# Shift columns by a selection matmul, v's shift rows behind the query stage, and the text modulated on its way out of PSUM

## The chip, the core and the metric

The kernel runs on one core of a Trainium2 chip. A core has five engines that work side by side and wait for one another through semaphores: TensorE multiplies matrices (PE in the profile; its loads of the stationary operand are PEld), VectorE (DVE) and ScalarE (ACT) work elementwise, GpSimd (POOL) does elementwise work more slowly and issues DMAs, and SyncE (SP) here issues most DMAs. Operands lie in SBUF, 128 partitions wide; TensorE writes its sums to PSUM, in banks of 512 fp32 values per partition. The metric is the device time of one execution in microseconds (us).

## What is computed

One attention block of a diffusion transformer with two streams, image and text. There are B = 2 batches, Ni = 256 image tokens and Nt = 32 text tokens in each, and D = 1152; all is bfloat16.

```python
mod_i = (_silu(c) @ wmod_img).reshape(B, 6, 1, D)      # only 0, 1, 2 are used
mod_t = (_silu(c) @ wmod_txt).reshape(B, 6, 1, D)
shi, sci, gai = mod_i[:, 0], mod_i[:, 1], mod_i[:, 2]  # shift, scale, gate; text likewise
hi = _layernorm(x_img, axis=-1) * (1 + sci) + shi
ht = _layernorm(x_txt, axis=-1) * (1 + sct) + sht
qkvi = hi @ wqkv_img
qkvt = ht @ wqkv_txt
# q, k, v: text tokens first, then image tokens
scores = jnp.einsum('bqd,bkd->bqk', q, k) * D ** (-0.5)
p = _softmax(scores, axis=-1)
a = jnp.einsum('bqk,bkd->bqd', p, v)
out_i = x_img + gai * (ai @ wo_img)
out_t = x_txt + gat * (at @ wo_txt)
```

## The kernel before, in words

**Tiling.** D is cut into KT = 9 blocks of 128; the 512 image tokens are NIT = 4 row blocks of 128, TPB = 2 for each batch. `hT_i` holds the modulated image tokens transposed (partitions: a block of D; columns: tokens). The text's 64 tokens are one tile, `xn_t`, and `hT_t` transposed.

**Weights.** Twelve blocks of 1152 x 1152 (2592 KB each) are used. They come on SP's queue in the order in which they stand in the code: `w_sc_i` and `w_v_i` in pieces between the rows of x, then `w_sh_i`, `w_q_i` (in thirds along D, `K3`), `w_sh_t`, `w_sc_t`, `w_k_i` (thirds), `x_t`, `w_q_t`, `w_k_t`, `w_ga_i`, `w_v_t`, `w_o_i`, `w_ga_t`, `w_o_t`. Their pool has six buffers that go round: `w_k_i` takes the place of `w_sc_i`, `w_q_t` that of `w_v_i`, `w_k_t` that of `w_sh_i`, `w_ga_i` that of `w_q_i`, and so on. A load is issued when the last reader of the tile that was there is done. SP works its queue in order.

**Stages.** The order of the instructions on each engine is the order of the code.
1. Layer norm of the image rows, transposes, scale. `mod_cols` (L188) makes modulation columns: for each block j of D, nine matmuls with a 128x128 block of weights as the stationary operand and the two columns of silu(c) moving, so 81 matmuls of two columns for all of D.
2. v of the image from hidden states that are scaled but not yet shifted (`v_block`, `v_rest`): v = (scaled x) @ w_v, with the shift's part, shift @ w_v, added to it later (`v_shift`, L393).
3. The shift's columns: `mod_cols(w_sh_i, ...)`, L347, copied to `mod_i` (L348) and, as bfloat16, to `shT32` (L349). `apply_mod` (L203) adds them to `hT_i`, nine slices for each batch, dealt over DVE, ACT and POOL.
4. `mod_rows` (L370) makes rows: the stationary operand is 32 columns wide, `sT32` or `shT32`, so four groups of matmuls share the array side by side (`tile_position`), each with 288 columns of the weights; the result has a row per group and batch, at partitions 32 g + b. The rows are written to DRAM by POOL (L385) and read back broadcast over partitions. For v's shift, `mod_rows(w_v_i, 4, lhs=shT32)` runs ahead of the query projection; the rows come back in `bvb` (L391).
5. `qk_img` (L410) for q and then k of the image: output blocks of 128 in groups, the first three together and then one by one; hooks put other work between groups. `v_shift` stands at block 5 of q. Behind q come the text's shift and scale rows (two `mod_rows`), which POOL reads back broadcast into `mb_t` (L433). In k's stage stand `txt_norm` (block 0), `txt_modulate` (block 5, L449 and L450 with `mb_t`) and `txt_transposes` (block 8; ACT copies the result to `hT_t`, L456).
6. Text q and k (L467), scores, softmax, the image's gate rows, text v, attention (`aps`), and the output projection: `out_chunk` (L643) for four row blocks, and between blocks 2 and 3 the text's gate and output. The output tile `o` has two buffers, and a stored block must land before its buffer is written again.

`evac` (L138) copies PSUM to SBUF in turn by DVE and ACT. Tiles of PSUM are seven buffers of `ps_mm` and one of `ps_sm`.

Of the kernel before, what the change touches and what calls it, by code (L numbers as in the profile page):

```python
# [14 lines left out]
def kernel(  # L15
# [14 lines left out]
    nc = tc.nc  # L30
    bf = mybir.dt.bfloat16
    f32 = mybir.dt.float32
    PSUM = bass.MemoryType.PSUM

    B, NI, D = x_img.shape
    NT = x_txt.shape[1]
    P = 128
    KT = D // P
    NTOK = NI + NT
    NIT = (B * NI) // P  # L40
    TPB = NI // P
    NTT = B * NT
# [8 lines left out]
    NM = 1024  # L51

    const = ctx.enter_context(tc.tile_pool(name="const", bufs=1))
    wpool = ctx.enter_context(tc.tile_pool(name="w", bufs=6))
    act = ctx.enter_context(tc.tile_pool(name="act", bufs=1))
    work = ctx.enter_context(tc.tile_pool(name="work", bufs=2))
    small = ctx.enter_context(tc.tile_pool(name="small", bufs=4))
    ps_mm = ctx.enter_context(tc.tile_pool(name="ps_mm", bufs=7, space=PSUM))
    ps_sm = ctx.enter_context(tc.tile_pool(name="ps_sm", bufs=1, space=PSUM))
# [13 lines left out]
    def load_w(src, c0, ksplits=((0, KT),)):  # L73
        t = wpool.tile([P, KT, D], bf, tag="w")
        for (k0, k1) in ksplits:
            nc.sync.dma_start(t[:, k0:k1, :], w_view(src)[:, k0:k1, c0:c0 + D])
        return t
# [6 lines left out]
    w_v_i = wpool.tile([P, KT, D], bf, tag="w", name="w_v_i")  # L84
# [22 lines left out]
    w_sh_i = load_w(wmod_img, 0)  # L107
    w_q_i = load_w(wqkv_img, 0, K3)


    ident = const.tile([P, P], bf)
# [5 lines left out]
    sT32 = const.tile([P, KT, 32], bf)  # L117
    nc.gpsimd.memset(sT32[:], 0.0)
    shT32 = const.tile([P, KT, 32], bf)
# [8 lines left out]
    sT = const.tile([P, KT, B], bf)  # L128
# [9 lines left out]
    def evac(out_ap, in_ap):  # L138
        if evac_idx[0] % 2 == 0:
            nc.vector.tensor_copy(out_ap, in_ap)  # L140
        else:
            nc.scalar.copy(out_ap, in_ap)
        evac_idx[0] += 1
# [20 lines left out]
    hT_i = act.tile([P, KT, B * NI], bf, tag="Bt")  # L164

    mod_i = const.tile([P, 2 * KT, B], f32, name="mod_img")
# [21 lines left out]
    def mod_cols(wt, out_ps, j0, j1):  # L188
        for j in range(j0, j1):
            for kt in range(KT):  # L190
                nc.tensor.matmul(out_ps[:, j - j0, :], lhsT=wt[:, kt, j * P:(j + 1) * P], rhs=sT[:, kt, :],  # L191
                                 start=(kt == 0), stop=(kt == KT - 1))
# [10 lines left out]
    def apply_mod(kt, t0, t1, shift, eng):  # L203
        b = t0 // TPB
        sl = hT_i[:, kt, t0 * P:t1 * P]
        ap = mod_i[:, kt, b:b + 1] if shift else mod_i[:, KT + kt, b:b + 1]
        op = ALU.add if shift else ALU.mult
        if eng == 0:
            nc.vector.tensor_scalar(sl, sl, ap, None, op0=op)
        elif eng == 1:  # L210
            if shift:
                nc.gpsimd.tensor_scalar(sl, sl, 1.0, ap, op0=ALU.mult, op1=ALU.add)
            else:
                nc.gpsimd.tensor_scalar(sl, sl, ap, 0.0, op0=ALU.mult, op1=ALU.add)  # L214
        elif shift:
            nc.scalar.activation(sl, sl, ACT.Identity, bias=ap, scale=1.0)
        else:
            nc.scalar.activation(sl, sl, ACT.Identity, scale=ap)
# [83 lines left out]
    v_i = act.tile([P, NIT, D], bf, tag="A")  # L302
# [26 lines left out]
    bvb = act.tile([P, B, D], bf)  # L329

    def v_rest(i0, i1):
        ps = ps_mm.tile([P, NIT, P], f32, tag="mm")
        for i in range(i0, i1):
            for kt in range(KT):
                nc.tensor.matmul(ps[:, i - i0, :], lhsT=hT_i[:, kt, i * P:(i + 1) * P], rhs=w_v_i[:, kt, NM:D],  # L335
                                 start=(kt == 0), stop=(kt == KT - 1))
        evac(v_i[:, i0:i1, NM:D], ps[:, 0:i1 - i0, :])

    v_rest(0, TPB)
    ps = ps_mm.tile([P, VW], f32, tag="mm")  # L340
    for kt in range(KT):
        nc.tensor.matmul(ps[:], lhsT=hT_i[:, kt, 3 * P:4 * P], rhs=w_v_i[:, kt, VW:NM], start=(kt == 0), stop=(kt == KT - 1))  # L342
    evac(v_i[:, 3, VW:NM], ps[:])


    mps = ps_sm.tile([P, KT, B], f32, tag="sm")
    mod_cols(w_sh_i, mps, 0, KT)  # L347
    nc.vector.tensor_copy(mod_i[:, 0:KT, :], mps[:])  # L348
    nc.scalar.copy(shT32[:, :, 0:B], mps[:])  # L349
    for kt in range(KT):  # L350
        apply_mod(kt, 0, TPB, True, (0, 1, 2, 0, 2, 1, 0, 0, 2)[kt])
    v_rest(TPB, NIT)

    w_sh_t = load_w(wmod_txt, 0)
    w_sc_t = load_w(wmod_txt, D)
    w_k_i = load_w(wqkv_img, D, K3)
# [7 lines left out]
    w_ga_t = load_w(wmod_txt, 2 * D)  # L364
    w_o_t = load_w(wo_txt, 0, K3)

    NGG = 4
    gsc = tc.dram_tile([5, B, D], bf, name="mod_scratch")

    def mod_rows(w_blk, si, add_one=False, lhs=None):  # L370
        lhs = sT32 if lhs is None else lhs
        gps = ps_mm.tile([P, VC], f32, tag="mm")
        for kt in range(KT):
            for g in range(NGG):
                nc.tensor.matmul(gps[32 * g:32 * g + 32, :], lhsT=lhs[:, kt, :], rhs=w_blk[:, kt, g * VC:(g + 1) * VC],  # L375
                                 start=(kt == 0), stop=(kt == KT - 1), tile_position=(0, 32 * g))
        g_sb = work.tile([P, VC], bf, tag="garow")
        if add_one:
            nc.vector.tensor_scalar_add(g_sb[:], gps[:], 1.0)
        else:  # L380
            evac(g_sb[:], gps[:])
        if si is None:
            return g_sb
        for b in range(B):
            nc.gpsimd.dma_start(gsc[si, b, :].rearrange("(g j) -> g j", g=NGG), g_sb[b:P:32, :])  # L385

    for kt in range(KT):
        apply_mod(kt, TPB, NIT, True, (0, 1, 2, 0, 2, 1, 0, 0, 2)[kt])
    mod_rows(w_v_i, 4, lhs=shT32)
    for b in range(B):  # L390
        nc.gpsimd.dma_start(bvb[:, b, :], gsc[4, b, :].partition_broadcast(P))  # L391

    def v_shift():  # L393
        for i in range(NIT):
            nc.vector.tensor_add(v_i[:, i, :], v_i[:, i, :], bvb[:, i // TPB, :])


    qkT = act.tile([P, 2 * KT, B, NTOK], bf, tag="Q")

# [10 lines left out]
    def qk_img(wq, blk, hooks):  # L410

        groups = [(0, 3)] + [(j, j + 1) for j in range(3, KT)]
        for (j0, j1) in groups:
            if j0 in hooks:
                hooks[j0]()
            pss = [ps_mm.tile([P, B * NI], f32, tag="mm", name="qkps") for _ in range(j0, j1)]
            for kt in range(KT):
                for j in range(j0, j1):
                    nc.tensor.matmul(pss[j - j0][:], lhsT=wq[:, kt, j * P:(j + 1) * P], rhs=hT_i[:, kt, :],  # L419
                                     start=(kt == 0), stop=(kt == KT - 1))  # L420
            for j in range(j0, j1):
                qk_evac(qkT[:, blk * KT + j, :, 0:NI], pss[j - j0][:].rearrange("p (b n) -> p b n", b=B), blk)

    mb_t = act.tile([NTT, 2, D], bf)

    def txt_rows_shift():
        mod_rows(w_sh_t, 0)

    def txt_rows_scale():
        mod_rows(w_sc_t, 1, add_one=True)  # L430
        for k in range(2):
            for b in range(B):
                nc.gpsimd.dma_start(mb_t[b * NT:(b + 1) * NT, k, :], gsc[k, b, :].partition_broadcast(NT))  # L433

    qk_img(w_q_i, 0, hooks={5: v_shift})
    txt_rows_shift()
    txt_rows_scale()

    hT_t = act.tile([P, KT, NTT], bf)

    xn_t = act.tile([NTT, D], bf)

    def txt_norm():
# [1 line left out]
        junk = small.tile([P, 1], f32, bufs=1)  # L445
        nc.scalar.activation(junk[:], eps_t[:], ACT.Exp)

    def txt_modulate():
        nc.vector.tensor_mul(xn_t[:], xn_t[:], mb_t[:, 1, :])  # L449
        nc.vector.tensor_add(xn_t[:], xn_t[:], mb_t[:, 0, :])  # L450

    def txt_transposes():
        tpt = ps_mm.tile([P, KT, NTT], bf, tag="mm")
        for kt in range(KT):
            nc.tensor.transpose(tpt[:, kt, :], xn_t[:, kt * P:(kt + 1) * P], ident[0:NTT, 0:NTT])
        nc.scalar.copy(hT_t[:], tpt[:])  # L456

    qk_img(w_k_i, 1, hooks={0: txt_norm, 5: txt_modulate, 8: txt_transposes})

    FG = 6  # L460
    for blk, wq in enumerate([w_q_t, w_k_t]):
        for j0 in range(0, KT, FG):
            jn = min(FG, KT - j0)
            ps = ps_mm.tile([P, FG, NTT], f32, tag="mm")
            for j in range(j0, j0 + jn):
                for kt in range(KT):
                    nc.tensor.matmul(ps[:, j - j0, :], lhsT=wq[:, kt, j * P:(j + 1) * P], rhs=hT_t[:, kt, :],  # L467
                                     start=(kt == 0), stop=(kt == KT - 1))
            qk_evac(qkT[:, blk * KT + j0:blk * KT + j0 + jn, :, NI:NTOK],
                    ps[:, 0:jn, :].rearrange("p j (b n) -> p j b n", b=B), blk)  # L470


    qpos = [[0, P, 2 * P], [NT, NT + P, 0]]
    rsum = {}
# [18 lines left out]
    def scores_txt_and_gate():  # L493
# [10 lines left out]
        for kt in range(KT):  # L504
            for g in range(NGG):
                c0 = 2 * VC + g * HC
# [6 lines left out]
        for b in range(B):  # L513
            nc.gpsimd.dma_start(gsc[3, b, 0:2 * VC].rearrange("(g j) -> g j", g=2), g_sb[64 + b:P:32, 0:VC])  # L514
            nc.scalar.dma_start(gsc[3, b, 2 * VC:D].rearrange("(g j) -> g j", g=NGG), g_sb[b:P:32, VC:VC + HC])
        return st
# [51 lines left out]
    def attn_out():  # L568
        for dts, own in (((0, 4, 1), 0), ((2, 5, 3), 1), ((6, 8, 7), 1)):
# [6 lines left out]
            for (dt, b, aps) in accs:  # L576
                g, blk = divmod(dt, NGG)
                r = 32 * (2 * (g % 2) + b)
# [43 lines left out]
    def txt_gate():  # L622
        g_sb = mod_rows(w_ga_t, None)
        return g_sb
# [72 lines left out]
    g_sb = txt_gate()  # L697
    pss = out_txt_mm()
# [37 lines left out]
```

## Time and profile before

| | us |
|---|---|
| median of 3 runs | 119.61 (119.52 to 120.07) |
| the profiled execution | 119.72 |
| its span, first to last instruction | 117.9 |
| busy in it: TensorE | 110.8 |
| busy: VectorE, ScalarE, GpSimd | 55.7, 33.0, 26.4 |
| moved by DMA | 41.63 MB, mean 353 GB/s |
| granted clock of TensorE | 1.00 |

The profile is of one execution. Its lines by engine give the busy time; the rows of slices cut the span in 40 equal parts of 2.95 us, with a digit for the busy tenths of each (9 is 90% or more) and, for DMA, the rate. The chain of waits is followed back from the last instruction: each piece has its start, its length and its name (engine, what it writes, line), with xN where N pieces were merged. In the timeline a row has the start, the length, the engine (a q behind it: the engine's instruction queue), the line and the operation, out<-in.

### The profile page before, as it was taken

The page shows a single profiled execution, that of the slowest core. Times are in us where ns is not written, and L with a number is a line of the kernel's source. Part 1 is how long each engine was busy: PE and PEld are TensorE (multiplying, and loading weights), DVE is VectorE, ACT ScalarE, POOL GpSimd, SP SyncE. Part 2 cuts the span into 40 slices and gives each one's busy share as a digit, 9 for nine tenths or more (in the row PEclk, how much of TensorE's full clock was granted, in tenths as well). Part 3 has the DMA queues.
Part 4 walks back from the last instruction along what each step waited for, and adds up shares of the span by engine and source line. Part 5 has one row for each costly group of instructions (what it writes and reads, how often), then busy time and mean ns, then how long its engine had stood idle before and what let it go on. Part 6 is the DMA issues. An engine that isn't in the chain of part 4 may idle for free.

```text
span 117.9 us, 2733 instructions
## 1 busy us (share of the span) xinstructions
PE 110.8 (94%) x1158; PEld 65.1 (55%) x1166; DVE 55.7 (47%) x131; ACT 33.0 (28%) x80; POOL 26.4 (22%) x53
## 2 busy tenths in 40 slices
PE   5858899999999999999999999999999999999990
PEld 1234564546964444455444447978665666667670
DVE  1789910452380221923362270336444778835781
ACT  4538660342090301220073032134533600000200
POOL 4000103700074020007070000002116089900000
DMA  3999999999999999999999999999999999991062
GB/s 77 347 392 349 366 323 382 413 411 412 405 412 407 407 411 413 411 408 334 356 408 402 331 411 413 403 416 399 414 401 411 417 381 399 410 370 49 0 183 67
DMA packets 22807, 41.63 MB, mean 353 GB/s; under 512 B 1231, under 2 KB 6507, under 8 KB 22795
## 3 DMA queue, kind: packets, MB, share of 16 engines
q1 hardware_dynamic: 21696, 39.68, 89.6%
q0 software_dynamic: 768, 1.64, 3.7%
q10 hardware_dynamic: 331, 0.15, 0.5%
q8 instruction: 9, 0.15, 0.5%
q14 instruction: 3, 0.02, 0.1%
HBM read 40.11 MB, written 1.35 MB: 352 GB/s over the span
## 4 chain that ended last, share of the span: by engine, by line
PE 75%; DVE 11%; DMA 9%; issue 1%; ACT 1%; DVEq 0%
PE qkps L419 30%; PE va L230 10%; PE ps L655 8%; DMA out_dram<-o 7%; DVE stats L149 5%; PE aps L573 4%; PE ps L467 4%; PE sps L487 4%; PE gps L375 3%; PE mps L191 3%; DMA x_i<-in_x_img_dram 3%; PE ps L588 2%; PE ps L335 2%; PE ps L342 2%; DVE tmp L662 2%; DVE xn_i L161 1%
## 5 line engine op out<-in xcount | busy, mean ns | idle before, releaser
L419 PE MATMUL qkps<-hT_i,t 128*128 128x512 bf16 x158 | 35.3, 379 | 0.2
L419 PEld LDWEIGHTS <-t 128*128 128x128 bf16 x162 | 15.6, 98 | 19.0 <-issue 0.5
L655 PE MATMUL ps<-t,aT 128*128 128x384 bf16 x99 | 16.4, 326 | 0.0
L230 PE MATMUL va<-w_v_i,hT_i 128*128 128x512 bf16 x60 | 14.1, 379 | 0.8 <-ACT hT_i L179 0.3
L655 PEld LDWEIGHTS <-aT 128*128 128x128 bf16 x117 | 11.1, 98 | 6.7 <-issue 0.2
L230 PEld LDWEIGHTS <-hT_i 128*128 128x128 bf16 x63 | 5.8, 97 | 7.2 <-issue 0.6
L639 POOL TENSOR_TENSOR w_og<-t,gb 128x384 bf16<-128x384 bf16 x9 | 8.7, 997 | 4.4 <-DMA gb<-mod_scratch 4.4
L662 DVE SCALAR_TENSOR_TENSOR tmp<-ps,rs,gb 128x384 bf16<-128x384 f32 x11 | 6.8, 617 | 2.4 <-PE ps L655 2.3
L149 DVE BATCH_NORM_STATS2 stats<-x_i 128x6 f32<-128x384 bf16 x12 | 6.0, 545 | 2.6 <-DMA x_i<-in_x_img_dram 2.6
L405 ACT ACTIVATE qkT<-qkps 128x512 bf16<-128x512 f32 x5 | 2.9, 596 | 14.4 <-PE qkps L419 14.4
L664 DVE TENSOR_TENSOR o<-tmp,x_i 128x384 bf16<-128x384 bf16 x11 | 5.1, 465 | 3.1 <-DMA out_dram<-o 2.7
L385 POOL DMA_DIRECT2D mod_scratch<-g_sb x6 | 3.6, 608 | 12.5 <-DVE g_sb L140 12.5
L214 POOL TENSOR_SCALAR hT_i<-hT_i,mod_img 128x256 bf16<-128x256 bf16 x5 | 2.5, 515 | 16.2 <-ACT rstd L156 9.6
L126 PE MATMUL wps<-wz 128*128 128x512 bf16 x14 | 4.9, 494 | 1.2 <-DVE wz L116 1.2
L403 DVE TENSOR_SCALAR qkT<-qkps 128x512 bf16<-128x512 f32 x4 | 2.7, 686 | 6.5 <-PE qkps L419 6.5
L514 POOL DMA_DIRECT2D mod_scratch<-g_sb x2 | 1.2, 582 | 19.9 <-DVE g_sb L511 19.9
L140 DVE CAST aT<-aps 128x288 bf16<-128x288 f32 x9 | 3.6, 451 | 3.3 <-PE aps L580 3.3
L467 PEld LDWEIGHTS <-t 128*128 128x128 bf16 x162 | 4.9, 98 | 0.2
L573 PE MATMUL aps<-pT,v_i 128*128 128x288 bf16 x36 | 4.9, 287 | 0.0
L467 PE MATMUL ps<-hT_t,t 128*128 128x64 bf16 x162 | 4.9, 193 | 0.0
L631 ACT CAST gbf<-bps 128x288 bf16<-128x288 f32 x2 | 0.7, 402 | 14.8 <-PE bps L629 14.8
L487 PE MATMUL sps<-qkT 128*128 128x288 bf16 x36 | 4.7, 286 | 0.0
(119 smaller groups left out, 135.6 us busy)
## 6 DMA issues: line engine op xcount, KB each, us to landing
t<-in_wmod_txt_dram SPq DMA_DIRECT2D x3, 2592.0 KB, 22.0
t<-in_wmod_img_dram SPq DMA_DIRECT2D x2, 2592.0 KB, 24.3
t<-in_wqkv_img_dram SPq DMA_DIRECT2D x6, 864.0 KB, 15.3
t<-in_wqkv_txt_dram SPq DMA_DIRECT2D x2, 2592.0 KB, 17.5
t<-in_wqkv_txt_dram SPq DMA_DIRECT2D x3, 864.0 KB, 13.5
t<-in_wo_img_dram SPq DMA_DIRECT2D x1, 2592.0 KB, 17.8
t<-in_wo_txt_dram SPq DMA_DIRECT2D x3, 864.0 KB, 15.2
w_sc_i<-in_wmod_img_dram SPq DMA_DIRECT2D x3, 576.0 KB, 7.6
```

What stands on the lines that cost most here:

```text
L126: nc.tensor.matmul(ps[:], lhsT=wz[:, 0:P], rhs=wz[:], start=True, stop=True)
L140: nc.vector.tensor_copy(out_ap, in_ap)
L149: nc.vector.bn_stats(stats[0:np_, k, :], x_ap[:, k * CH:(k + 1) * CH])
L230: nc.tensor.matmul(ps[:], lhsT=hT_i[:, kt, i * P:(i + 1) * P], rhs=w_v_i[:, kt, half * VW:(half + 1) * VW], start=(kt == 0), stop=(kt == K ...
L419: nc.tensor.matmul(pss[j - j0][:], lhsT=wq[:, kt, j * P:(j + 1) * P], rhs=hT_i[:, kt, :], start=(kt == 0), stop=(kt == KT - 1))
L467: nc.tensor.matmul(ps[:, j - j0, :], lhsT=wq[:, kt, j * P:(j + 1) * P], rhs=hT_t[:, kt, :], start=(kt == 0), stop=(kt == KT - 1))
L487: nc.tensor.matmul(sps[:], lhsT=qkT[:, ft, b, q0:q0 + P], rhs=qkT[:, KT + ft, b, :], start=(ft == 0), stop=(ft == KT - 1))
L573: nc.tensor.matmul(aps[:], lhsT=v_i[:, b * TPB + kj, dt * P:(dt + 1) * P], rhs=pTs[b][:, kj, :], start=(kj == 0), stop=False)
L639: nc.gpsimd.tensor_mul(w_og[:, dt, 0:CH], w_o_i[:, dt, NG0:D], gb[:, B - 1, NG0:D])
L655: nc.tensor.matmul(ps[:, 0:cw], lhsT=aT[:, dt, t0:t0 + P], rhs=rhs, start=(dt == DTS[0]), stop=(dt == DTS[-1]))
L662: nc.vector.scalar_tensor_tensor(tmp[:, 0:cw], ps[:, 0:cw], rsum[(b, qi)][:], gb[:, b, cs], op0=ALU.mult, op1=ALU.mult)
L664: nc.vector.tensor_add(o[:, cs], tmp[:, 0:cw], x_i[:, i, cs])
```

## The change

- Shift columns: `rows_for_cols` makes the shift as rows, four groups side by side with 256 columns each, for the first eight blocks of D. An evacuation puts the rows in SBUF (`shr`). `select_cols` then turns rows into columns: the stationary operand is a 128x128 block of `shr`, the moving one is `sel8`, which holds the eight columns of the identity that belong to the rows in use; two matmuls of eight columns. The ninth block's column comes from nine matmuls as before (`last_col`). `cols_out` writes the columns to `mod_i` by two DVE operations.
- Order in front: v's last columns of the second batch come first; those of the first batch stand around the selection, one row block before it and one behind. `apply_mod` takes batch 1 first, then batch 0; q's first group of three blocks goes over the tokens in two cuts, batch 1 and then batch 0. `shT32` is copied by POOL.
- v's shift rows, with their DMAs, come behind the query stage and the text's rows. `v_shift` is done for row blocks 0 and 1 on POOL, placed at block 8 of k, and for 2 and 3 on DVE, behind the text's q and k.
- Text: shift and scale are made as rows and turned into columns too (`txt_cols`, at block 3 of k); the way over DRAM and `mb_t` is gone. The transposes of the normalized text stand at block 5, and DVE multiplies and adds as it moves the result from PSUM to `hT_t`.

The diff, cut:

```diff
-    v_rest(0, TPB)
+    sel8 = const.tile([P, NGG, B], bf)
+    nc.gpsimd.tensor_copy(sel8[:], ident[:].rearrange("p (g r) -> p g r", g=NGG)[:, :, 0:B])
+    def rows_for_cols(wt, nm):
+        gps = ps_mm.tile([P, RC], f32, tag="mm")
+        for kt in range(KT):
+            for g in range(NGG):
+                nc.tensor.matmul(gps[32 * g:32 * g + 32, :], lhsT=sT32[:, kt, :], rhs=wt[:, kt, g * RC:(g + 1) * RC],
+                                 start=(kt == 0), stop=(kt == KT - 1), tile_position=(0, 32 * g))
+        g_sb = work.tile([P, RC], bf, tag=nm, bufs=1, name=nm)
+        evac(g_sb[:], gps[:])
+        return g_sb
+    def last_col(wt, cps):
+        for kt in range(KT):
+            nc.tensor.matmul(cps[:, NCOL:NCOL + B], lhsT=wt[:, kt, (KT - 1) * P:D], rhs=sT[:, kt, :],
+                             start=(kt == 0), stop=(kt == KT - 1))
+    def select_cols(g_sb, cps):
+        for c in range(2):
+            nc.tensor.matmul(cps[:, c * NGG * B:(c + 1) * NGG * B], lhsT=g_sb[:, c * P:(c + 1) * P],
+                             rhs=sel8[:].rearrange("p g b -> p (g b)"), start=True, stop=True)
+    def cols_out(dst, cps, add):
+        nc.vector.tensor_scalar_add(dst[:, 0:KT - 1, :].rearrange("p (g c) b -> p c g b", c=2),
+                                    cps[:, 0:NCOL].rearrange("p (c g b) -> p c g b", c=2, b=B), add)
+        nc.vector.tensor_scalar_add(dst[:, KT - 1, :], cps[:, NCOL:NCOL + B], add)
+    v_rest(TPB, NIT)
...
-    mod_cols(w_sh_i, mps, 0, KT)
-    nc.vector.tensor_copy(mod_i[:, 0:KT, :], mps[:])
-    nc.scalar.copy(shT32[:, :, 0:B], mps[:])
+    shr = rows_for_cols(w_sh_i, "shr")
+    cps = ps_sm.tile([P, NCOL + B], f32, tag="sm")
+    last_col(w_sh_i, cps)
+    psr = ps_mm.tile([P, TPB, P], f32, tag="mm")
+    for i in range(TPB):
+        for kt in range(KT):
+            nc.tensor.matmul(psr[:, i, :], lhsT=hT_i[:, kt, i * P:(i + 1) * P], rhs=w_v_i[:, kt, NM:D],
+                             start=(kt == 0), stop=(kt == KT - 1))
+        if i == 0:
+            select_cols(shr, cps)
+            cols_out(mod_i[:, 0:KT, :], cps, 0.0)
     for kt in range(KT):
-        apply_mod(kt, 0, TPB, True, (0, 1, 2, 0, 2, 1, 0, 0, 2)[kt])
-    v_rest(TPB, NIT)
+        apply_mod(kt, TPB, NIT, True, SHE[kt])
+    evac(v_i[:, 0:TPB, NM:D], psr[:])
+    nc.gpsimd.tensor_copy(shT32[:, :, 0:B], mod_i[:, 0:KT, :])
+    for kt in range(KT):
+        apply_mod(kt, 0, TPB, True, SHE[kt])
...
-    mod_rows(w_v_i, 4, lhs=shT32)
-    for b in range(B):
-        nc.gpsimd.dma_start(bvb[:, b, :], gsc[4, b, :].partition_broadcast(P))
...
+            cuts = [(NI, B * NI), (0, NI)] if blk == 0 and j0 == 0 else [(0, B * NI)]
...
-    qk_img(w_q_i, 0, hooks={5: v_shift})
-    txt_rows_shift()
-    txt_rows_scale()
+    qk_img(w_q_i, 0, hooks={})
+    tsh = rows_for_cols(w_sh_t, "tsh")
+    tsc = rows_for_cols(w_sc_t, "tsc")
+    mod_rows(w_v_i, 4, lhs=shT32)
+    for b in range(B):
+        nc.gpsimd.dma_start(bvb[:, b, :], gsc[4, b, :].partition_broadcast(P))
+    ctp = ps_sm.tile([P, 2, NCOL + B], f32, tag="sm")
+    last_col(w_sh_t, ctp[:, 0, :])
+    last_col(w_sc_t, ctp[:, 1, :])
...
-        nc.vector.tensor_mul(xn_t[:], xn_t[:], mb_t[:, 1, :])
-        nc.vector.tensor_add(xn_t[:], xn_t[:], mb_t[:, 0, :])
...
-        nc.scalar.copy(hT_t[:], tpt[:])
+        nc.vector.tensor_mul(hv, tpt[:].rearrange("p k (b t) -> p k b t", b=B),
+                             mod_t[:, 1, :, :].unsqueeze(3).to_broadcast([P, KT, B, NT]))
+        nc.vector.tensor_add(hv, hv, mod_t[:, 0, :, :].unsqueeze(3).to_broadcast([P, KT, B, NT]))
...
-    qk_img(w_k_i, 1, hooks={0: txt_norm, 5: txt_modulate, 8: txt_transposes})
+    qk_img(w_k_i, 1, hooks={0: txt_norm, 3: txt_cols, 5: txt_transposes, 8: shift_two})
...
+    for i in range(2, NIT):
+        v_shift(i, nc.vector)
```

More of the change, by code (lines that the diff above doesn't have):

```diff
@@ L337, in v_rest @@
         evac(v_i[:, i0:i1, NM:D], ps[:, 0:i1 - i0, :])
-    v_rest(0, TPB)
+    NGG = 4
+    RC = 2 * P
+    sel8 = const.tile([P, NGG, B], bf)
+    nc.gpsimd.tensor_copy(sel8[:], ident[:].rearrange("p (g r) -> p g r", g=NGG)[:, :, 0:B])
+    NCOL = 2 * NGG * B
+    def rows_for_cols(wt, nm):
[20 more added lines that the diff above has]
+    v_rest(TPB, NIT)
     ps = ps_mm.tile([P, VW], f32, tag="mm")
@@ L343 @@
     evac(v_i[:, 3, VW:NM], ps[:])
-    mps = ps_sm.tile([P, KT, B], f32, tag="sm")
-    mod_cols(w_sh_i, mps, 0, KT)
-    nc.vector.tensor_copy(mod_i[:, 0:KT, :], mps[:])
-    nc.scalar.copy(shT32[:, :, 0:B], mps[:])
-    for kt in range(KT):
-        apply_mod(kt, 0, TPB, True, (0, 1, 2, 0, 2, 1, 0, 0, 2)[kt])
-    v_rest(TPB, NIT)
+    shr = rows_for_cols(w_sh_i, "shr")
[9 more added lines that the diff above has]
+            cols_out(mod_i[:, 0:KT, :], cps, 0.0)
+    SHE = (0, 1, 2, 0, 2, 1, 0, 0, 2)
+    for kt in range(KT):
+        apply_mod(kt, TPB, NIT, True, SHE[kt])
[3 more added lines that the diff above has]
+        apply_mod(kt, 0, TPB, True, SHE[kt])
     w_sh_t = load_w(wmod_txt, 0)
@@ L365 @@
     w_o_t = load_w(wo_txt, 0, K3)
-    NGG = 4
     gsc = tc.dram_tile([5, B, D], bf, name="mod_scratch")
@@ L385, in mod_rows, with v_shift @@
             nc.gpsimd.dma_start(gsc[si, b, :].rearrange("(g j) -> g j", g=NGG), g_sb[b:P:32, :])
-    for kt in range(KT):
-        apply_mod(kt, TPB, NIT, True, (0, 1, 2, 0, 2, 1, 0, 0, 2)[kt])
-    mod_rows(w_v_i, 4, lhs=shT32)
-    for b in range(B):
-        nc.gpsimd.dma_start(bvb[:, b, :], gsc[4, b, :].partition_broadcast(P))
-    def v_shift():
-        for i in range(NIT):
-            nc.vector.tensor_add(v_i[:, i, :], v_i[:, i, :], bvb[:, i // TPB, :])
+    def v_shift(i, eng):
+        eng.tensor_add(v_i[:, i, :], v_i[:, i, :], bvb[:, i // TPB, :])
     qkT = act.tile([P, 2 * KT, B, NTOK], bf, tag="Q")
@@ L416, in qk_img @@
             pss = [ps_mm.tile([P, B * NI], f32, tag="mm", name="qkps") for _ in range(j0, j1)]
[L417 to L420, printed above, removed]
+            cuts = [(NI, B * NI), (0, NI)] if blk == 0 and j0 == 0 else [(0, B * NI)]
+            for (t0, t1) in cuts:
+                for kt in range(KT):
+                    for j in range(j0, j1):
+                        nc.tensor.matmul(pss[j - j0][:, t0:t1], lhsT=wq[:, kt, j * P:(j + 1) * P],
+                                         rhs=hT_i[:, kt, t0:t1], start=(kt == 0), stop=(kt == KT - 1))
             for j in range(j0, j1):
                 qk_evac(qkT[:, blk * KT + j, :, 0:NI], pss[j - j0][:].rearrange("p (b n) -> p b n", b=B), blk)
[L424 to L433, printed above, removed]
-    qk_img(w_q_i, 0, hooks={5: v_shift})
-    txt_rows_shift()
-    txt_rows_scale()
+    qk_img(w_q_i, 0, hooks={})
[7 more added lines that the diff above has]
+    last_col(w_sc_t, ctp[:, 1, :])
+    mod_t = const.tile([P, 2, KT, B], f32, name="mod_txt")
     hT_t = act.tile([P, KT, NTT], bf)
@@ L446, in txt_norm, with txt_cols @@
         nc.scalar.activation(junk[:], eps_t[:], ACT.Exp)
-    def txt_modulate():
-        nc.vector.tensor_mul(xn_t[:], xn_t[:], mb_t[:, 1, :])
-        nc.vector.tensor_add(xn_t[:], xn_t[:], mb_t[:, 0, :])
+    def txt_cols():
+        select_cols(tsh, ctp[:, 0, :])
+        select_cols(tsc, ctp[:, 1, :])
+        for k in range(2):
+            cols_out(mod_t[:, k, :, :], ctp[:, k, :], float(k))
     def txt_transposes():
@@ L455, in txt_transposes, with shift_two @@
             nc.tensor.transpose(tpt[:, kt, :], xn_t[:, kt * P:(kt + 1) * P], ident[0:NTT, 0:NTT])
-        nc.scalar.copy(hT_t[:], tpt[:])
-    qk_img(w_k_i, 1, hooks={0: txt_norm, 5: txt_modulate, 8: txt_transposes})
+        hv = hT_t[:].rearrange("p k (b t) -> p k b t", b=B)
+        nc.vector.tensor_mul(hv, tpt[:].rearrange("p k (b t) -> p k b t", b=B),
+                             mod_t[:, 1, :, :].unsqueeze(3).to_broadcast([P, KT, B, NT]))
+        nc.vector.tensor_add(hv, hv, mod_t[:, 0, :, :].unsqueeze(3).to_broadcast([P, KT, B, NT]))
+    def shift_two():
+        for i in range(2):
+            v_shift(i, nc.gpsimd)
+    qk_img(w_k_i, 1, hooks={0: txt_norm, 3: txt_cols, 5: txt_transposes, 8: shift_two})
     FG = 6
```

## The prediction

> **What bounds the kernel now.** First the page: how busy is TensorE, and how busy are the DMA engines, slice by slice?
>
> ```profile
> PE 110.8 (94%) x1158; PEld 65.1 (55%) x1166; DVE 55.7 (47%) x131; ACT 33.0 (28%) x80; POOL 26.4 (22%) x53
> PE   5858899999999999999999999999999999999990
> DMA  3999999999999999999999999999999999991062
> GB/s 77 347 392 349 366 323 382 413 411 412 405 412 407 407 411 413 411 408 334 356 408 402 331 411 413 403 416 399 414 401 411 417 381 399 410 370 49 0 183 67
> ```
>
> Both are full, from about 10 to 106 us. So there are two clocks: the matmuls, and the weights on SP's queue. Which decides is read where the stream ends, in the chain from 93 us on.
>
> ```profile
> 98.84 8.05 DMA out_dram<-o
> 106.99 0.36 DVE o L664
> 108.18 0.47 DVE g_sb L140
> 108.69 0.40 PE bps L629 x2
> ```
>
> The first image row block's store lies behind the last weights and lands at 106.9; DVE needs its buffer, and the gate rows' evacuation stands behind that. But the text matmuls before L629 (36 in 2.25 from 106.22) would have let TensorE go on at about 108.55. So the transfers lead by 0.14 us: a later stream moves the end fully, a later TensorE all but 0.14, and speeding up one of them alone wins at most that.
>
> Next, the chain from 28 to 55 us, where the change works.
>
> ```profile
> 30.02 2.02 PE mps L191 x81
> 32.03 1.03 PE ps L335 x18
> 33.06 1.22 PE gps L375 x36
> 34.28 0.32 PE qkps L419
> ...
> 51.87 2.32 PE gps L375 x72
> ```
>
> No wait appears: the 81 small matmuls for the shift's columns, 18 for v's last columns, 36 for v's shift rows, the query projection, and the text's two sets of rows.
>
> Last, SP's part of the timeline.
>
> ```profile
> 44.97 2.00 SPq L358 DMA_DIRECT2D x_t<-in_x_txt_dram  x1
> 47.07 6.85 SPq L76 DMA_DIRECT2D t<-in_wqkv_txt_dram  x2
> 54.02 7.70 SPq L76 DMA_DIRECT2D t<-in_wmod_img_dram  x1
> ```
>
> SP runs from one issue to the next; it is held by a full queue, not by buffers. w_q_t, issued at 47.07, lands at 64.58.
>
> **TensorE, step by step** (times of this profiled execution: 119.72 us, span 117.9 with 1.8 around it; the median of the runs is 119.61, so the change found is added to that).
>
> Front, from 30.02. Out: 2.02 + 1.03 + 1.22 = 4.27. In:
> - shift rows, 36 matmuls of 256 columns: 1.22 x 256/288 = 1.08.
> - last block's column, 9 x 2.02/81 = 0.22; v's last columns of the first row block, 1.03/2 = 0.5. Together they hide ACT's evacuation (an L142 of 128x256 took 0.36).
> - two selections: nothing like them is in the trace; from 0.05 (two of L191's) to 0.2 (two of the spread, L629, 0.40 for 2 x 288 columns, are dearer). I take 0.1, as they have 8 columns. TensorE is at 31.9.
> - then DVE: two column operations (L348: 0.18) and a shift of 128x256 (L209: 0.29), with three handovers of 0.05: first shifted slice at about 32.75. The second half of v's columns covers 0.5 of it; 0.4 is open. DVE's queue holds nothing else then; POOL (0.55 a slice) and ACT (0.50) keep ahead of the 3 x 0.109 that TensorE needs for a slice.
>
> So the query projection starts at 32.8, not 34.28. Its first three blocks come in two cuts of 27 matmuls of 256 columns (54 x 0.109 against 27 x 0.217: nothing). But it now meets its weights. The second third of w_q_i lands at 33.07; the last one, 885 KB at the 410 GB/s of the page, is due 2.16 later, at 35.2. TensorE asks for it after 18 matmuls, at 34.76: a wait of 0.45, which also swallows whatever is won ahead of it. Then 36 x 0.109 and 54 x 0.217: the query stage ends at 50.9 instead of 51.87, 1.0 early.
>
> Then text shift and scale rows, 2 x 1.03, v's shift rows 1.16, two last columns 18 x 0.025 = 0.46, entry and exit of the column tiling 0.1: 3.8 in place of 2.32. The key projection starts 0.5 later than before. Four selections in it: 0.1. Text transposes stay 0.36, and move three blocks ahead. In all +0.6 (from -0.25, the bare count of matmuls with every wait hidden, to +1.0, with both waits whole and dearer selections); at the end 0.14 less: +0.45.
>
> Edits at no price, with their cover: DVE's multiply and add of the text as it leaves PSUM replace two of 0.75 and ACT's copy of 0.64; three key blocks (6 us) cover them, and without that cover up to 1.5 would show. v's shifts 2 and 3 (L395, 0.75 each) stand on DVE between the last text evacuation (76.8) and the first row maximum (78.1): the maximum is some 0.2 late, but the transposes that follow wait for it only at 83. On POOL, shifts 0 and 1 are priced by L639 (997 ns for 384 columns): 3 us each, after the broadcast rows land near 66, done by 73; POOL's next duty, the gate rows' DMAs, comes at 81.8. The four column operations of the text (0.18 each) take DVE 0.7 near 60, while TensorE has four more PSUM buffers to fill. v's shift rows take their DMAs along: two small writes and two broadcasts of 288 KB, 0.6 each to issue on POOL (L385, L391), which idles there, and whose eight text issues go. shT32's copy moves to POOL, where nothing follows but batch 0's slices, due 3 us later.
>
> POOL's long additions can hold up DVE: L664 takes 357 ns at the least and 750 at the most, beside L639, so 0.4 more against a POOL addition of 1.0. By that row a text add beside a POOL shift costs at most 1.2 more, within the 6 us of cover. A rule speaks against this part: the Trainium skill, "SBUF — State Buffer", section "Who interferes with whom", says that VectorE and GpSimd take a shared port by an exclusive lock and that a tensor_tensor with two SBUF inputs contends; by it the text add could be shut out for a whole shift, which would leave the sum as it is only because of the same cover.
>
> **The transfers.** Out: four loads of text modulation (4 x 72 KB, 0.295 MB at 410 GB/s: 0.7 us). The four small writes ahead of them are nothing. bvb's 0.59 MB (1.4 us) moves from 44-47 to after 60.
>
> The cost is in a buffer. The pool holds six weight tiles, so w_q_t takes w_v_i's place, and w_v_i is read last by v's shift rows: before at 34, now behind the query stage and the text rows, 50.9 + 0.1 + 2.06 + 1.16 = 54.2. SP, whose issue stood at 47.07, waits seven us, and every later weight load is queued behind it. What covers it is the backlog. Summing the bytes of SP's queue in the order of issue, what precedes w_q_t is through at 55.2 now, and at 53.8 with bvb gone from before it. The first packet follows an issue by 0.3 (the store at 111.90: bytes by 112.4) to 1.0 (the first load at 0.74: nothing by 1.70). So the stream restarts at 54.7 to 55.4, dry for 0.9 to 1.6. Less the 0.7 saved: +0.2 to +0.9 at the end; I take +0.5, a little below the middle, since the queue is warm. If engines that lag (landings come 1.3 to 2.3 after the sum of bytes) use the pause to catch up, it is less, down to -0.7 at best.
>
> The Trainium skill, "DMA: Bandwidth & Descriptors", section "Anatomy of one DMA", puts a fixed 2.0 us on a DMA, mostly completion. Here a 32 KB store takes 1.5 from issue to landing, and its first bytes come early, as the page says. Had all 2.0 stood ahead of the bytes, the stream would be 1.7 later.
>
> Both clocks thus lose about half a us; the later one decides, and small waits where they cross (w_ga_i lands at 78.31 for 79.12; w_v_t's last third at 84.76 for 85.35) can add a little: **+0.65, 120.3 us**, from +0.3 to +1.3.
>
> **Rivals.**
> - *The stream falls far behind*: SP released later, or a slow restart; dry for 2.4 rather than 1.3, so +1.7, and TensorE then waits for w_ga_i. 121.3 us, up to 121.6. For it: the margin is thin and every load is behind it. Against: packets of the warm queue came within 0.5 us.
> - *It ends even*: the ring's lag is caught up in the pause, and w_q_i's third lands by 34.8. TensorE then starts the key stage +0.1 to +0.2; +0.2 in all: 119.8. For it: landings vary by 1 us against the bytes.
> - *Not slower but faster*: 70 matmuls fewer in the front and fewer bytes count whole. The place is the handover after the selection: if it hides (the first shifted slice by 32.4 and the weights by 34.3) TensorE gains its bare 0.25, the transfers give 0.7, and the end is 0.14 + 0.25 = 0.4 early: 119.2. Only with the key stage starting before 54.0 does it decide. The landing of w_q_i's third speaks against it; to pass 119.0 more would have to go.
>
> **How the numbers follow.** Forecast 0.50, far behind 0.17, even 0.22, faster 0.11. About 0.5% (0.6 us: below 119.0, above 120.2) is what a measurement can tell. Slower: 0.38 of the forecast's 0.50, whose middle lies just beyond the limit, and all of 0.17: 0.55. Faster: half of the last rival and a little for what I overlooked, 0.07. The rest, 0.38, is the same. The range 119.4 to 121.4 leaves out a tenth on each side.
>
> **What would show it.** Right: SP's w_q_t issue at about 54 with a buffer wait; a slice of GB/s near 54 to 56 below 300; a TensorE wait near 35 for w_q_i; query stage ending near 50.9, key stage starting near 54.7; the first store landing after 107. Wrong: w_q_t issued near 47; a key stage that starts before 54.1; text operations or the late shifts on the chain; an end above 121.4 or below 119.4.

## The result, and the profile after

The changed kernel takes 124.03 us (median of 4 runs, 122.86 to 124.75) against 119.65: 3.1% slower, ratio 1.0312 with a 95% interval of 1.0266 to 1.0357. One of its four runs (124.75) counts as slow, and the ratio leaves it out. 120.3 was forecast, in a range of 119.4 to 121.4. The profiled execution took 122.86, its span is 121.1.

From the page of the kernel after, the rows for busy TensorE, the DMA engines and their rate in 40 slices:

```profile
PE 111.3 (92%) x1173; PEld 67.4 (56%) x1181; DVE 54.9 (45%) x134; ACT 32.8 (27%) x79; POOL 26.9 (22%) x49
PE   5768999999969999999999999999999999997980
DMA  3999999999999999999999999999999999991052
GB/s 88 346 377 337 322 347 380 394 390 390 391 394 385 395 388 389 391 393 292 368 391 397 405 387 394 394 388 390 393 390 390 391 340 392 391 362 60 2 177 68
```

The DMA engines are as busy as before, but a busy slice moves 390 GB/s, where it moved 411. That begins in the eighth slice, near 21 us, where the code of both kernels is still the same: everything up to line 334 is. TensorE has one dent, in the twelfth slice.

The chain of waits of the kernel after, at the end:

```profile
101.36 8.24 DMA out_dram<-o
109.69 0.36 DVE o L706
110.97 0.38 DVE g_sb L140
111.39 0.41 PE bps L671 x2
```

The same pieces as before, 2.5 to 2.8 later (109.69 for 106.99, 111.39 for 108.69): the transfers' clock decides, and by more. SP's queue moves 39.68 MB in all; 37.2 of them are weights, since the list in the account of the kernel before has fourteen blocks and not twelve. All of it takes 39.68/0.391 = 101.5 us at the new rate and 39.68/0.411 = 96.5 at the old: some 5 more, an estimate. In the trace the last weights land at 108.84, where they landed at 106.16: 2.7 later, although the change has 0.29 MB less to move.

The chain around the front:

```profile
36.41 4.32 PE qkps L453 x37
...
52.17 2.08 PE gps L349 x72
54.25 1.10 PE gps L415 x36
55.35 0.53 PE ctp L357 x18
```

Its piece before 36.41 is the load of `w_q_i`: the wait that was forecast, 1.09 us instead of 0.45 on the slower stream. And SP's part of the timeline:

```profile
44.99 2.14 SPq L399 DMA_DIRECT2D x_t<-in_x_txt_dram  x1
47.23 7.03 SPq L76 DMA_DIRECT2D t<-in_wqkv_txt_dram  x2
55.40 6.39 SPq L76 DMA_DIRECT2D t<-in_wmod_img_dram  x1
```

w_q_t is issued at 47.23, as before. The wait that the prediction put there does not exist. (The second load of that row, w_k_t, and then w_ga_i do wait for their buffers; more on that below.)

### The profile page after: what moved, and what is told of

The parts are those of the page before. It is cut to its first block, busy times and chain, and to the rows that moved or that the text cites. A ratio compares the mean times of both kernels' runs of the same rounds, so it can differ in the third digit from the quotient of the medians.

```text
span 121.1 us, 2752 instructions
## 1 busy us (share of the span) xinstructions
PE 111.3 (92%) x1173; PEld 67.4 (56%) x1181; DVE 54.9 (45%) x134; ACT 32.8 (27%) x79; POOL 26.9 (22%) x49
## 3 DMA queue, kind: packets, MB, share of 16 engines
q1 hardware_dynamic: 21696, 39.68, 91.8%
## 4 chain that ended last, share of the span: by engine, by line
PE 56%; DMA 19%; SPq 17%; DVE 4%; issue 1%; DVEq 0%
PE qkps L453 27%; DMA t<-in_wqkv_img_dram 12%; SPq L95 8%; PE ps L697 7%; DMA out_dram<-o 7%; SPq L76 5%; PE aps L615 4%; PE ps L506 4%; PE sps L529 4%; SPq L87 2%; PE gps L349 2%; PE ps L630 2%; DVE o L706 2%; SPq L91 1%; DVE tmp L704 1%
## 5 line engine op out<-in xcount | busy, mean ns | idle before, releaser
L453 PE MATMUL qkps<-hT_i,t 128*128 128x512 bf16 (+1 forms) x185 | 35.7, 348 | 1.4 <-DMA t<-in_wqkv_img_dram 1.1
L453 PEld LDWEIGHTS <-t 128*128 128x128 bf16 x189 | 18.1, 98 | 17.5 <-DMA t<-in_wqkv_img_dram 1.6
L425 POOL DMA_DIRECT2D mod_scratch<-g_sb x2 | 1.4, 690 | 21.3 <-DVE g_sb L140 21.3
L428 POOL TENSOR_TENSOR v_i<-v_i,bvb 128x1152 bf16<-128x1152 bf16 x2 | 4.7, 2364 | 4.8 <-DMA bvb<-mod_scratch 4.8
L142 ACT CAST qkT<-qkps 128x512 bf16<-128x512 f32 x5 | 2.8, 582 | 10.0 <-PE qkps L453 10.0
L140 DVE CAST qkT<-qkps 128x512 bf16<-128x512 f32 x4 | 2.8, 692 | 5.4 <-PE qkps L453 5.4
L506 PEld LDWEIGHTS <-t 128*128 128x128 bf16 x162 | 4.9, 98 | 0.2
```

The costliest lines, as they stand in the source:

```text
L453: nc.tensor.matmul(pss[j - j0][:, t0:t1], lhsT=wq[:, kt, j * P:(j + 1) * P], rhs=hT_i[:, kt, t0:t1], start=(kt == 0), stop=(kt == KT - 1))
```

## The experiments: why is the stream slower from 20 us on?

What differs there is not code but addresses. The change adds two constants to the pool `const`, `sel8` (16 bytes a partition, which take 32) and `mod_txt` (144, which take 160). The weights' pool stands behind them. In the built program's list of tiles, before, x and the weight tiles begin at multiples of 256 bytes of a partition (the first weight tile at 19712); in the changed one at 192 past a multiple (19904). A weight row is 2304 bytes, nine times 256, so all rows keep the offset of the first. The first four kernels ran together on one chip and the last two on two others, each time with the kernel before beside them (119.89 to 119.93).

**The changed kernel as it is** (`after_again`):

> The changed kernel as it is, on the same chip as the three beside it. If the slow weight stream (packets of 2304 bytes in 95 to 107 ns instead of 93, 390 GB/s instead of 412, from the first microseconds on) belongs to the program, it is there again and the time is 122.8 to 124.8 us. If it belonged to the chip or the hour, the stream runs at 410 and the time is 119.5 to 120.5.

**The changed kernel, tiles aligned** (`after_base0`):

```diff
     eps_t = const.tile([P, 1], f32)
     nc.vector.memset(eps_t[:], EPS)
+    pad_t = const.tile([P, 32], bf)
+    nc.vector.memset(pad_t[:], 0.0)
```

> The changed kernel with 64 bytes of padding among the small constants, so that x and the weight tiles begin on a multiple of 256 bytes again, as in the kernel before (19712); the change's two new constants had moved them to 192 past one (19904). Theory, the start addresses slow the stream: packets back at 93 ns, 410 GB/s, the first store lands near 106.2 (0.7 less than before, for the text's loads that are gone), and the end is TensorE's: 119.9 to 120.5 us. Rival, the stream is slowed by the change's own order of loads and waits: still 122.8 to 124.8.

**The kernel before, tiles moved by 192 bytes** (`before_base192`; the same two lines with 96 columns):

> The kernel before with 192 bytes of padding among the small constants and nothing else: x and the weight tiles begin 192 past a multiple of 256, where they stand in the changed kernel. Theory, start addresses: packets of 95 to 107 ns, 390 GB/s, 122.8 to 124.5 us. Rival, the change's own work: no difference, 119.5 to 120.1.

**The kernel before, tiles moved by 256 bytes** (`before_base256`; 128 columns):

> The kernel before with 256 bytes of padding: the same tiles are moved too, but again begin on a multiple of 256. Theory, start addresses within 256 bytes: no difference, 119.5 to 120.1 us with packets of 93 ns. If any move of the tiles slows the stream: 122 or more.

**Moved by 64 bytes** (`before_base64`; 32 columns):

> The kernel before with 64 bytes of padding: x and the weight tiles begin 64 past a multiple of 256. At 192 past it, packets took 99 ns instead of 93 and the time rose by 5.3 us. Theory one, the cost grows with the offset: a third of it here, packets of 95, about 121.7 us. Theory two, any start off the multiple costs the same: packets of 99, about 125. The Trainium skill, "DMA: Bandwidth & Descriptors", section "How a descriptor splits into AXI transactions", counts beats: 72 for an aligned 2304 bytes, 74 at 64 past, 78 at 192 past, which is theory one.

**Moved by 128 bytes** (`before_base128`; 64 columns):

> The kernel before with 128 bytes of padding: the tiles begin 128 past a multiple of 256. At 64 and at 192 past it the cost was the same, 5.1 and 5.3 us. Theory, any start off 256 costs an added piece per row: 125. Rival, a multiple of 128 is enough: 119.9.

| kernel | start past a multiple of 256 | us, median | ratio to before (95%) | packet of 2304 bytes, mean ns (19 to 52 us) |
|---|---|---|---|---|
| before | 0 | 119.9 | 1 | 93.4 |
| before_base256 | 0 | 119.80 | 0.9996 (0.9973 to 1.0020) | 93.3 |
| before_base64 | 64 | 125.05 | 1.0432 (1.0398 to 1.0465) | 98.5 |
| before_base128 | 128 | 125.14 | 1.0436 (1.0392 to 1.0480) | 98.9 |
| before_base192 | 192 | 125.15 | 1.0443 (1.0399 to 1.0487) | 98.6 |
| after_again | 192 | 123.81 | 1.0325 (1.0281 to 1.0369) | 99.1 |
| after_base0 | 0 | 120.44 | 1.0040 (1.0019 to 1.0060) | 93.3 |

The view of the stretch from 20 to 32 us gives the length, the busy times of TensorE, its weight loads, VectorE, ScalarE and GpSimd with their counts, the granted clock, the DMA share and GB/s. The kernel before:

```profile
20.00:32.00 12.00, 11.87 (x165) 7.51 (x166) 4.33 (x8) 3.04 (x6) 2.23 (x10) 1.00 1.04 410
```

The kernel before moved by 192:

```profile
20.00:32.00 12.00, 11.69 (x133) 6.68 (x134) 4.33 (x8) 3.04 (x6) 2.22 (x10) 1.00 1.06 393
```

The changed kernel:

```profile
20.00:32.00 12.00, 11.87 (x134) 6.78 (x135) 4.33 (x8) 3.41 (x7) 2.36 (x11) 1.00 1.06 392
```

The changed kernel, aligned:

```profile
20.00:32.00 12.00, 11.87 (x143) 7.15 (x143) 4.43 (x9) 3.41 (x7) 2.35 (x11) 1.00 1.04 410
```

Start addresses alone slow the kernel before by 5.1 to 5.3 us, and 64 bytes of padding give the changed kernel 3.4 of its 3.9 us on this chip back. It is not the chip, nor being moved as such (256 costs nothing), nor the change's order of loads. The cost is a step, not a slope: 64, 128 and 192 cost the same, 6% per row on average, so the theory of a cost that grows with the offset fell. (Aligned, at least 99% of the rows take exactly 93 ns; moved, most take between 93 and 108, most often 95, 100 or 107.)

The Trainium skill, "DMA: Bandwidth & Descriptors", section "How a descriptor splits into AXI transactions", has a rule of this kind: an aligned descriptor is cut in pieces of 256 bytes, and one that starts elsewhere costs extra beats, for bytes that are fetched and not used. The runs agree that 256 is the line, as far as they go: 0 and 256 are fast, 64, 128 and 192 slow. But here only the place that is written was moved, and the cost is not what one would estimate from the page's beats of 32 bytes, 74/72 at 64 past and 78/72 at 192 past.

On the bad addresses the change is even a gain, 123.8 against 125.15: there the transfers decide, and it moves fewer bytes (0.29 MB, 0.75 us at 392 GB/s). The rest of the 1.3 was not taken apart.

## The experiments: what the change itself costs

With the tiles aligned the changed kernel is 0.4% slower, 0.55 us. Three kernels, aligned too, take it apart by the prediction's two clocks.

**The text's part alone** (`text_alone`: front, v's shift rows and `v_shift` as before):

> The kernel before, tiles aligned, with the text part of the change alone (rows to columns by the selection, multiplied and added on the way out of PSUM; no way over DRAM). By the two clocks: TensorE 0.3 later, the transfers 0.7 shorter, TensorE decides: +0.15, 120.0 to 120.2. Rival, the transfers decide all along: -0.7, 119.2.

**The front alone** (`front_alone`: text as before, v's shift rows ahead of q):

> The kernel before, tiles aligned, with the front part alone: the selection, the order of batches, v's shift rows ahead of the query stage as before, the text as before. By the two clocks: TensorE 0.6 early, the transfers unchanged and now alone at the end: within 0.15 of before, 119.8 to 119.9. Rival, TensorE decides: -0.6, 119.3.

**Front and text, v's shift rows ahead of q** (`front_text_rows_early`), against the changed kernel, cut (tiles aligned as above; `shift_two` and the two late `v_shift` are gone):

```diff
+    nc.scalar.copy(shT32[:, :, 0:B], mod_i[:, 0:KT, :])
     for kt in range(KT):
         apply_mod(kt, TPB, NIT, True, SHE[kt])
...
-    nc.gpsimd.tensor_copy(shT32[:, :, 0:B], mod_i[:, 0:KT, :])
...
+    mod_rows(w_v_i, 4, lhs=shT32)
+    for b in range(B):
+        nc.gpsimd.dma_start(bvb[:, b, :], gsc[4, b, :].partition_broadcast(P))
-    qk_img(w_q_i, 0, hooks={})
+    qk_img(w_q_i, 0, hooks={5: lambda: [v_shift(i, nc.vector) for i in range(NIT)]})
     tsh = rows_for_cols(w_sh_t, "tsh")
     tsc = rows_for_cols(w_sc_t, "tsc")
-    mod_rows(w_v_i, 4, lhs=shT32)
-    for b in range(B):
-        nc.gpsimd.dma_start(bvb[:, b, :], gsc[4, b, :].partition_broadcast(P))
```

> The changed kernel with the tiles aligned and v's shift rows back ahead of the query stage (ScalarE copies the columns for them), v's shifts all on VectorE at block 5 of q as before; the selection in front and the text's new way stay. By the prediction's two clocks: TensorE gains 0.6 in front and the rows' 1.2 fill what was the wait for the query weights; the text costs it 0.3; the transfers save 0.7. The end is 0.4 early: 119.4 to 119.6 against 119.9. Rival, the wait only moves (to the copy ahead of the rows, or to the weights): 119.9 to 120.4.

Measured: text alone 120.49 (ratio 1.0061, 1.0039 to 1.0084), the front alone 120.07 (1.0021, 0.9995 to 1.0048), front and text with early rows 120.08 (1.0023, 0.9997 to 1.0049). The front fits: 0.14 above the kernel before, and the interval includes no difference. The two with the text's new way are 0.3 to 0.7 above what was expected. The chain of the third shows that the front did what was worked out:

```profile
29.86 1.10 PE gps L351 x36
30.96 0.31 PE cps L359 x9
...
31.79 0.05 PE cps L364 x2
...
31.86 0.18 DVE mod_img L368
32.04 0.08 DVE mod_img L370
...
32.15 0.30 DVE hT_i L211
...
32.45 1.29 PE gps L417 x36
33.74 17.66 PE qkps L459 x108
```

From the selection to the first shifted slice it is 0.6; the early rows then fill what was a wait, and q starts at 33.74 (34.28 in the kernel before). Its last vector operation is

```profile
114.75 0.35 DVE o L701
```

and that of the kernel before

```profile
115.01 0.35 DVE o L658
```

so it ends 0.26 earlier, at 115.10. Yet its span is 0.23 longer. So the loss is behind the last store: 1.59 us from its landing to the end of the span, where the kernel before has 1.09. What SP waits for there, in the kernel before:

```profile
SPq L731 <- PEq L731: 0.7, 2, 0.5
```

and in the changed kernel, aligned:

```profile
SPq L775 <- PEq L775: 1.1, 2, 0.5
```

That is the closing barrier, where all engines meet. In it GpSimd stands still for 0.4 us once: in `after_base0` between its first and second instruction of the barrier, in the text kernels, whose GpSimd program has three instructions less, between the fourth and fifth. A stall at a fixed place in a program looks like its code being fetched. Three kernels test that.

**Eight GpSimd instructions more** (`front_text_pool8`, against `front_text_rows_early`):

```diff
+    for _ in range(8):
+        nc.gpsimd.memset(pad_t[:], 0.0)
     v_t = act.tile([P, VW], bf)
```

> The version with the front selection, early rows and the text's new way, tiles aligned, plus eight small memsets on GpSimd near 23 us, where it is idle. That version's last vector operation ended 0.26 earlier than that of the kernel before, but its span was 0.3 longer: in the closing barrier GpSimd stood still for 0.39 between two of its instructions, and three instructions earlier in the program of a kernel with three more GpSimd instructions. Theory: a refill of GpSimd's code at a fixed place in its program, which the fewer instructions let fall into the closing barrier; eight more move it ahead of the barrier. Tail after the last store 1.1 instead of 1.59, time 119.5 to 119.7 against 119.9. Rival, the stall belongs to what the change does at the end: no difference, 120.1.

**The changed kernel, aligned, four more** (`after_base0_pool4`):

> The changed kernel, tiles aligned, plus four of the same memsets on GpSimd. Theory, the code refill: tail 1.1 instead of 1.49, so 120.0 to 120.1 instead of 120.44. Rival, all of its 0.55 is TensorE's: 120.4.

**The kernel before, six GpSimd instructions less** (`before_pool6less`):

```diff
-                nc.gpsimd.tensor_copy(selF[:, r, g, b, :], ident[:, col:col + 1].to_broadcast([P, NT]))
+                eng = nc.gpsimd if r == 0 and g == 0 else nc.vector
+                eng.tensor_copy(selF[:, r, g, b, :], ident[:, col:col + 1].to_broadcast([P, NT]))
```

> The kernel before with six of the eight copies for the text gate's selection made by VectorE, so that GpSimd has six instructions fewer, as in the changed kernel. Theory, the code refill: tail 1.49 instead of 1.09, 120.2 to 120.4. Rival: no difference, 119.8 to 120.0.

| kernel | GpSimd instructions, as recorded | last store to end, us | median, us | ratio (95%) |
|---|---|---|---|---|
| before | 80 | 1.09 | 119.93 | 1 |
| front_alone | 81 | 1.09 | 120.07 | 1.0021 (0.9995 to 1.0048) |
| front_text_pool8 | 78 | 1.09 | 119.63 | 0.9979 (0.9951 to 1.0008) |
| after_base0_pool4 | 77 | 1.09 | 120.16 | 1.0008 (0.9987 to 1.0030) |
| after_base0 | 74 | 1.49 | 120.44 | 1.0040 (1.0019 to 1.0060) |
| before_pool6less | 74 | 1.50 | 120.13 | 1.0017 (0.9995 to 1.0040) |
| front_text_rows_early | 71 | 1.59 | 120.08 | 1.0023 (0.9997 to 1.0049) |
| text_alone | 71 | 1.58 | 120.49 | 1.0061 (1.0039 to 1.0084) |

With 77 instructions or more the stall is gone from the barrier, with 74 or fewer it is in it, whatever they do. The other six profiles agree: the four moved versions of the kernel before have 80 and 1.09, the two of the changed kernel as it is 74 and 1.49 to 1.52. A tail of 1.58 instead of 1.09 is also about what the two text kernels had above their sums. The tails in the traces settle it. The times, 0.2 to 0.45 us apart, do not by themselves: the two versions with added instructions ran on another chip than those without, and the intervals overlap. The profiled execution of `after_base0_pool4` is not even shorter (span 118.7), since its last store lands 0.5 later than that of `after_base0`. Where the barrier is free of the stall, it has a place that costs nothing: GpSimd's queue reaches its last wait 0.58 to 0.61 us after the first addition for `w_og` begins, and 0.24 in the kernels with a long tail; nine additions of about 1 us cover the difference. That the stall is a code fetch is not shown. The four kernels with a long tail have an 8 KB instruction transfer at the end of the span or up to 0.3 us behind it (118.4 to 119.2), the four with a short one at 98.1 to 99.2 instead. So something of the code moves with the stall; but that transfer begins 0.7 us or more after the stall is over, so it is not what GpSimd waited for.

The fastest version is `front_text_pool8`, 119.63 against 119.93; the interval includes no difference, so it is not shown to beat the kernel before.

## Why the prediction was wrong

**The step that failed is one that is not in it.** The new constants were counted as nothing, since they take no time on an engine; that they move the tiles behind them was not considered, and every transfer, w_q_i's last third and the whole stream, was priced at the 410 GB/s of the kernel before. The missing term: 6% on the stream, some 5 us by the rates; at the landing of the last weights 4.05 us (108.84 in the changed kernel, 104.79 in `after_base0`), and 3.4 in the time (`after_again` to `after_base0`). That the tiles move could have been read beforehand: 192 bytes more ahead of a pool whose tiles began at a multiple of 256. What that costs no run had shown.

**The named danger was not there.** The buffers do not go round in the order of the code, as the account of the kernel before and the prediction's paragraph on the transfers have it, but in the order in which tiles are released. By the programs' addresses w_q_t always takes `w_sh_i`'s place. In the changed kernel w_k_t takes w_q_i's and w_ga_i takes w_v_i's, so SP does wait, at 45.9 to 50.8 and 52.0 to 54.0 in `after_base0`, but with w_q_t's 2592 KB still queued; its lowest slice there has 320 GB/s, where the kernel before had 334. The forecast slice below 300 is there in the changed kernel, the nineteenth with 292, but without the wait that was to cause it: w_q_t is in the queue by 47.9, and the kernel before dips at the same place. The rival "the stream falls far behind" named the right clock with the wrong cause. Two details in the prediction's part on the transfers do not hold either: 54.2 with 0.3 to 1.0 gives 54.5 to 55.2, not 54.7 to 55.4; and the section that it cites for a fixed 2.0 us is on DMAs that GpSimd issues, while the weights and the store beside it are on SP's queue.

**TensorE's sum held.** The chain of `after_base0`:

```profile
35.06 4.32 PE qkps L455 x37
...
50.81 2.08 PE gps L351 x72
52.89 1.10 PE gps L417 x36
54.00 0.54 PE ctp L359 x18
54.53 0.67 PE qkps L455 x3
...
105.48 1.22 PE gps L417 x36
106.70 2.33 PE ops L720 x36
109.02 0.35 PE bps L673 x2
```

The wait for w_q_i's last third ends at 35.06 (35.2 was worked out) after 0.40 (0.45); the query stage ends at 50.81 (50.9); rows and columns behind it take 3.72 (3.8). The key stage starts 0.35 later than before (0.5), and L673, the spread of the gate, 0.33 later (0.45). With the tail's 0.4 that makes the 0.7 by which the spans differ (118.6 and 117.9); the medians differ by 0.55, of which `after_base0_pool4` keeps 0.2. The tail was in no term either. That the aligned kernel's 120.44 comes so near the forecast 120.3 is in part luck: the transfers' half us was not there, and the tail's 0.4 stands where it was expected.

**The transfers' saving was mis-sized**: the last weights land at 104.79 in `after_base0` and at 106.16 in the profile of before, 1.4 early (1.2 against `before_base256`) instead of 0.7 for the bytes. The rest goes with a slow stretch that came with the text's loads: 64 to 67 us in the kernel before,

```profile
64.00:67.00 3.00, 2.95 (x15) 1.37 (x14) 0.00 (x0) 0.59 (x1) 0.00 (x0) 1.00 1.05 320
```

and in `text_alone`, without those loads:

```profile
64.00:67.00 3.00, 3.00 (x22) 1.41 (x21) 2.11 (x3) 0.00 (x0) 0.00 (x0) 1.00 1.04 411
```

That the loads themselves slow it, rather than their small packets, was not tried. On aligned tiles TensorE then decides at the end (no transfer is left in the chain's last lines), and this gain is not seen. v's late shifts, POOL's long additions and the text's new evacuation cost nothing, as forecast: none of them is on the chain. Whether VectorE and GpSimd would have shut each other out was hardly tried: in `after_base0` the text's add ends at 66.32, and POOL's first shift begins at 66.19.

## What to carry to other kernels

Before trusting a comparison, look at the stretch in which both kernels run the same code: if the rate differs there, the cause is not an operation but where things lie. A kernel that streams weights should fix the alignment of its DMA targets (here 256 bytes) and not leave it to the sum of its small constants. When transfers and TensorE end within 0.2 us of each other, a part that helps one of them shows nothing until the other is helped too.

## What was not expected of the hardware

- Rows of 2304 bytes that begin 64, 128 or 192 bytes past a multiple of 256 in SBUF take 98.5 to 99 ns on a DMA engine on average, aligned ones 93.4; 410 GB/s become 392. This is measured for the weights on SP's queue. For the broadcasts on POOL's queue (packets of 4608 bytes) a tile's own address does not settle it. `bvb` begins 64 past a multiple in the kernel before and takes 178 ns (median), the same as `gb`, which begins on one. In the kernel before moved by 64, `gb` begins 64 past and takes 193; moved by 192, `bvb` begins on a multiple and takes 181. Why is open.
- The number of GpSimd instructions, whatever they do, moves a stall of 0.4 us into or out of the closing barrier.
